# Two chunks of one batch, instead of one chunk of two batches, in the first paired tiles of a linear attention with a gated feed-forward on one core

## The chip, the core and the metric

The kernel runs on one core of a Trainium2 chip. The metric is the device time of one execution in microseconds (us). A profile is one execution recorded by the hardware profiler; its span runs from the first to the last instruction.

## What is computed

The reference has two parts. The first is a linear attention with a decaying state, for 4 batches, 8 heads, 768 tokens and a head dimension of 48:

```python
for t in range(S):
    cur = np.einsum('bhd,bhe->bhde', u[None] * kt, vt)
    y[:, :, t] = np.einsum('bhd,bhde->bhe', rt, state + cur)
    state = wt[:, :, :, None] * state + np.einsum('bhd,bhe->bhde', kt, vt)
```

The second takes the 3072 rows of 384 values that this gives, scales each by its root mean square and a gain, and computes `(silu(xn @ w_gate) * (xn @ w_val)) @ w_out` with an inner width of 1536. Everything comes and goes as float32.

## The kernel before, in words

**Tiles.** The 768 tokens of a batch are cut into 6 chunks of 128. A tile (n, j) is chunk n of batch j: 24 tiles. For each tile the attention is done in matrix form: the logarithms of the decay are summed along the tokens with a triangular matrix (`cs_mm`), the sums are exponentiated (`exp_r`, `exp_k`), r and k are multiplied by them (`r_mul`, `k_mul`) into the buffer `rk`, `rk` is transposed (`rk_pe` on TensorE and `rk_tr`, a copy out of PSUM; or a transposing DMA from chunk 2 on), a score matrix is formed (`q_mm`), masked (`q_mask_e`, `q_mask_o`), and multiplied by v (`y_mm`), together with the state that the chunks before left (`st_mm`, `st_new`). A term for the token itself (`bonus_mul`, `bonus_sum`, `bonus_v`, mostly GpSimd's work) is added in `x_add`. `x_sq`, `x_rstd`, `xn_mul` normalise the row, `xn_pe` and `xn_out` transpose it into `xnt`, the input of the feed-forward.

**Feed-forward.** Four tiles make one group of 512 tokens. A group has 12 units; each is a `gate_mm` and a `val_mm` (3 matmuls of 512 columns each, line 741), a `silu` on ScalarE, and an `h_mul` on VectorE into `ht`. Then come four `o_mm` of 12 matmuls (line 784), `o_out` and `out_dma`. In the groups of the tuple `HALF` (0 and 1) a unit is computed for two tiles at a time: 6 matmuls of 256 columns (line 746), so that it needs only half of the group's tiles. The table `COL` says which tile has which place in which group: group 0 holds chunks 0 and 1 of batches 0 and 1.

**Pairs.** The four tiles in `PAIR` = (0,0), (0,1), (1,0), (1,1) are laid out specially. The loaded data of chunk n of batches 0 and 1 lie in one tile: batch 0 on partitions 0 to 63, batch 1 on 64 to 127, two neighbouring tokens on a partition, so that a descriptor moves 384 bytes instead of 192. Each load (`load` line 276, `load_w` line 298) therefore fills 64 partitions, and it takes two for each of w, r, k and v of a chunk: 16 loads of 192 KB. All later tiles load 128 partitions with 192-byte rows (lines 280 and 298), and w of chunks 0 and 1 of batches 2 and 3 (`WIN`) two tokens a partition on 128 partitions, 384 KB at once.

**Order.** One string, `ORDER`, lists all steps as name.n.j; the program issues them in that order, and every engine works through its own part strictly in sequence. All loads are on SyncE's (SP's) queue. The weights `wg_sb` and `wv_sb` (in two parts: units 0 to 3, and units 4 to 11) and `wo` are loaded by GpSimd's queue (lines 394 and 399). PSUM is used in rings: two banks for gate and for the sums of r ("a"), two for val and the sums of k ("b"), four for the rest ("q").

Of the kernel before, what the change touches and what calls it, by code (L numbers as in the profile page):

```python
# [25 lines left out]
u_mm.0.0 load_w.0.1 load_w.0.0 load_r.0.0 load_k.1.0 load_k.0.1 load_r.0.1 ln.0.0 u_out.0.0 cs_mm.0.1 load_k.0.0  # L26
exp_r.0.1 cs_mm.0.0 load_w.1.0 load_w.1.1 load_r.1.0 load_k.1.1 exp_k.0.1 exp_r.0.0 r_mul.0.1 exp_k.0.0 bonus_mul.0.1
bonus_mul.0.0 ln.1.0 k_mul.0.1 r_mul.0.0 w_tot.0.0 w_tot.0.1 k_mul.0.0 rk_pe.0.1 g_mm.0.0 rk_pe.0.0 cs_mm.1.0
load_r.1.1 rk_tr.0.1 exp_r.1.0 load_v.0.1 load_w.0.3 load_v.0.0 cs_mm.1.1 load_w.0.2 exp_k.1.0 rk_tr.0.0 bonus_sum.0.1
r_mul.1.0 exp_r.1.1 exp_k.1.1 g_out.0.0 w_tot.1.1 k_mul.1.0 q_mm.0.0 bonus_mul.1.1 k_mul.1.1 load_gv.0.1 q_mask_e.0.0  # L30
rk_pe.1.0 q_mm.0.1 ln.0.3 load_v.1.0 load_v.1.1 load_k.0.3 load_r.0.3 bonus_mul.1.0 bonus_sum.0.0 r_mul.1.1 cast_v.0.1
cast_v.0.0 q_mask_o.0.0 q_mask_o.0.1 q_mask_e.0.1 cs_mm.0.3 bonus_v.0.0 st_mm.0.0 st_mm.0.1 rk_pe.1.1 st_new.0.0
bonus_v.0.1 y_mm.0.0 ln.0.2 rk_tr.1.0 rk_tr.1.1 w_tot.1.0 st_new.0.1 load_gv.0.0 bonus_sum.1.0 x_add.0.0 bonus_sum.1.1
y_mm.0.1 load_r.0.2 exp_r.0.3 q_mm.1.1 cast_v.1.0 cast_v.1.1 x_sq.0.0 x_rstd.0.0 w_tot.0.3 x_add.0.1 q_mm.1.0
bonus_v.1.0 load_gv.1.0 q_mask_e.1.1 q_mask_o.1.1 bonus_v.1.1 xn_mul.0.0 x_sq.0.1 exp_k.0.3 load_k.0.2 cs_mm.0.2
st_mm.1.0 q_mask_e.1.0 q_mask_o.1.0 xn_pe.0.0 y_mm.1.1 r_mul.0.3 exp_r.0.2 x_rstd.0.1 xn_mul.0.1 exp_k.0.2 xn_out.0.0
xn_pe.0.1 w_tot.0.2 x_add.1.1 load_v.0.2 bonus_mul.0.3 k_mul.0.3 x_sq.1.1 y_mm.1.0 x_rstd.1.1 xn_out.0.1 load_gv.1.1
x_add.1.0 load_w.2.0 load_k.1.2 xn_mul.1.1 load_r.1.2 r_mul.0.2 st_new.1.0 load_v.0.3 x_sq.1.0 load_w.2.2 x_rstd.1.0
bonus_mul.0.2 gate_mm.0.0 rk_pe.0.3 st_mm.1.1 xn_pe.1.1 val_mm.0.1 k_mul.0.2 gate_mm.0.1 rk_pe.0.2 xn_mul.1.0
load_r.1.3 load_v.1.2 load_k.1.3 silu.0.1 silu.0.0 rk_tr.0.3 xn_pe.1.0 val_mm.0.0 cast_v.0.2 load_w.2.1 gate_mm.0.3  # L40
# [80 lines left out]
gate_mm.5.9 val_mm.5.2 val_mm.5.4 gate_mm.5.5 h_mul.5.2 silu.5.5 silu.5.9 o_out.4.3 val_mm.5.9 out_dma.4.2 h_mul.5.4  # L121
val_mm.5.5 gate_mm.5.7 gate_mm.5.10 h_mul.5.9 h_mul.5.5 out_dma.4.3 val_mm.5.7 silu.5.7 silu.5.10 val_mm.5.10
h_mul.5.7 o_out.4.1 h_mul.5.10 o_mm.5.0 o_mm.5.3 o_mm.5.2 o_out.5.3 o_mm.5.1 o_out.5.0 out_dma.5.3 out_dma.5.0
out_dma.4.1 o_out.5.2 out_dma.5.2 o_out.5.1 o_mm.5.4 out_dma.5.1 o_out.5.4 out_dma.5.4
"""


@with_exitstack
def kernel(
# [13 lines left out]
    nc = tc.nc  # L143
# [700 lines left out]
```

## Time and profile before

| | |
|---|---|
| time, median of 3 runs | 205.45 us (204.31 to 205.63) |
| time of the profiled execution | 204.67 us |
| its span | 203.0 us |
| busy: PE, VectorE (DVE), ScalarE (ACT), GpSimd (POOL) | 189.7, 155.5, 137.7, 123.2 us |
| mean granted TensorE clock | 0.991 |
| DMA traffic | 32.44 MB, mean 160 GB/s |

In the profile PE is TensorE's matmul stream; matmuls are pipelined, so the time between the starts of two of them is the price of one, and not the duration that is shown. `ps_au`, `ps_qx` and so on are PSUM banks of the rings a, b and q. In the chain of waits each row is a piece of the work that ended last: start, length, what. In a timeline row the square bracket says how long the engine had been idle before it and what released it.

### The profile page before, as it was taken

To read this page: it belongs to the slowest core of one execution; us is meant where nothing else is said; L and a number is where in the kernel's file an instruction comes from. 1 tells how busy PE (TensorE), PEld (TensorE's weight loads), DVE (VectorE), ACT (ScalarE), POOL (GpSimd) and SP (SyncE) were. 2 spreads that over 40 slices of the span, in tenths; PEclk is the share of its full clock that TensorE was granted. 3 is DMA by queue.
4 is the path that set the end of the run, shared out by engine and by line. 5 is a ranking of instruction groups with operands and counts; after the bars stand their busy time and mean duration, and the time that the engine had idled before them with its cause. 6 is when DMAs were issued, how large, how long until landed. Compare 5 with 4: busy or idle time off the path is not lost.

```text
span 203.0 us, 4914 instructions
## 1 busy us (share of the span) xinstructions
PE 189.7 (93%) x1832; PEld 128.2 (63%) x1832; DVE 155.5 (77%) x304; ACT 137.7 (68%) x282; POOL 123.2 (61%) x178
## 2 busy tenths in 40 slices
PE   2798779999999999999999997999999999999993
PEld 0356569989768999765556663556655565555562
DVE  6279896799988999988999987899898892044611
ACT  2547996689988667988598969667886484063500
POOL 7299992294639985486998198558797474300000
PEclk9999988999999999999999999999999999999999
DMA  5999999999999999999999989991367112001122
GB/s 121 218 226 248 192 209 211 188 196 168 210 208 204 183 208 210 191 214 204 235 204 204 207 202 211 217 185 39 100 111 196 39 30 72 19 17 63 39 97 99
DMA packets 115520, 32.44 MB, mean 160 GB/s; under 512 B 110372, under 2 KB 114344, under 8 KB 115496
## 3 DMA queue, kind: packets, MB, share of 16 engines
q1 hardware_dynamic: 113456, 28.58, 68.4%
q0 software_dynamic: 2032, 3.54, 10.0%
q8 instruction: 14, 0.23, 0.5%
q14 instruction: 10, 0.08, 0.1%
q10 hardware_dynamic: 8, 0.00, 0.0%
HBM read 25.96 MB, written 4.72 MB: 151 GB/s over the span
## 4 chain that ended last, share of the span: by engine, by line
PE 62%; DMA 13%; POOL 10%; ACT 6%; SPq 5%; issue 3%; POOLq 0%; ACTq 0%
PE ps_au L741 6%; PE ps_av L741 6%; PE ps_bu L741 5%; PE ps_bv L741 5%; PE ps_qz L784 5%; PE ps_av L746 4%; PE ps_au L746 4%; DMA wt<-in_w_dram 4%; PE ps_qx L784 4%; PE ps_qv L784 4%; PE ps_bu L746 4%; POOL ruk L535 4%; PE ps_bv L746 3%; DMA wg_sb<-in_moe_w_gate_dram 3%; POOL ruk L536 3%; PE ps_qu L784 3%
## 5 line engine op out<-in xcount | busy, mean ns | idle before, releaser
L784 PEld LDWEIGHTS <-ht 128*128 128x128 bf16 x300 | 28.5, 98 | 17.0
L253 ACT ACTIVATE sg<-ps_au 128x512 bf16<-128x512 f32 x35 | 20.9, 598 | 16.9 <-PE ps_au L741 9.1
L253 ACT ACTIVATE sg<-ps_av 128x512 bf16<-128x512 f32 x37 | 22.1, 596 | 15.1 <-PE ps_av L741 12.8
L770 DVE TENSOR_TENSOR ht<-ps_bu,sg 128x512 bf16<-128x512 f32 x24 | 16.5, 686 | 14.0 <-PE ps_bu L741 10.9
L536 POOL TENSOR_TENSOR ruk<-ruk,u_bc 128x384 f32<-128x384 f32 x24 | 24.3, 1011 | 1.9
L741 PEld LDWEIGHTS <-wg_sb 128*128 128x128 bf16 x144 | 15.5, 114 | 14.1 <-issue 1.6
L741 PEld LDWEIGHTS <-wv_sb 128*128 128x128 bf16 x144 | 15.5, 114 | 13.0
L741 PE MATMUL ps_av<-xnt,wg_sb 128*128 128x512 bf16 x75 | 20.3, 379 | 1.3 <-ACT sg L253 1.3
L770 DVE TENSOR_TENSOR ht<-ps_bv,sg 128x512 bf16<-128x512 f32 x24 | 16.4, 685 | 6.3 <-PE ps_bv L741 3.9
L545 POOL TENSOR_TENSOR ydiag<-vt,diag 128x384 f32<-128x384 f32 x20 | 16.5, 831 | 7.3 <-DVE diag L540 5.4
L535 POOL TENSOR_TENSOR ruk<-rt,kt 128x384 f32<-128x384 f32 x20 | 20.0, 1002 | 0.2 <-DMA rt<-in_r_dram 0.2
L741 PE MATMUL ps_bu<-xnt,wv_sb 128*128 128x512 bf16 x72 | 19.5, 380 | 0.0
L741 PE MATMUL ps_bv<-xnt,wv_sb 128*128 128x512 bf16 x72 | 19.5, 380 | 0.0
L784 PE MATMUL ps_qv<-wo,ht 128*128 128x384 bf16 x108 | 19.0, 326 | 0.0
L741 PE MATMUL ps_au<-xnt,wg_sb 128*128 128x512 bf16 x69 | 18.7, 380 | 0.0
L253 ACT ACTIVATE lw<-wt 128x384 bf16<-128x384 f32 (+1 forms) x20 | 11.5, 583 | 7.8 <-DMA wt<-in_w_dram 7.8
L251 ACT ACT_TABLE_LOAD x12 | 15.4, 1283 | 1.8 <-PEq L828 1.6
L529 POOL TENSOR_TENSOR rk<-kt,ek 128x384 bf16<-128x384 f32 x15 | 15.2, 1024 | 2.3 <-DMA kt<-in_k_dram 2.3
L746 PEld LDWEIGHTS <-wg_sb 128*128 128x128 bf16 x144 | 15.5, 115 | 1.5 <-DMA wg_sb<-in_moe_w_gate_dram 0.9
L746 PEld LDWEIGHTS <-wv_sb 128*128 128x128 bf16 x144 | 15.2, 114 | 0.4
L695 ACT ACTIVATE xn<-xb,rstd 128x384 bf16<-128x384 f32 x24 | 14.3, 611 | 1.0 <-POOL rstd L691 0.8
L682 ACT ACTIVATE junk<-xb 128x384 bf16<-128x384 f32 x24 | 12.4, 518 | 1.7 <-DVE xb L677 1.5
(210 smaller groups left out, 445.4 us busy)
## 6 DMA issues: line engine op xcount, KB each, us to landing
wt<-in_w_dram SPq DMA_DIRECT2D x20, 192.0 KB, 3.8
kt<-in_k_dram SPq DMA_DIRECT2D x20, 192.0 KB, 3.8
rt<-in_r_dram SPq DMA_DIRECT2D x20, 192.0 KB, 4.3
vt<-in_v_dram SPq DMA_DIRECT2D x20, 192.0 KB, 3.8
out_dram<-ob SPq DMA_DIRECT2D x19, 192.0 KB, 2.2
wo<-in_moe_w_out_dram POOLq DMA_DIRECT2D x3, 384.0 KB, 6.7
out_dram<-ob SPq DMA_DIRECT2D x10, 96.0 KB, 2.8
ht<-in_r_dram SPq DMA_DIRECT2D x4, 192.0 KB, 5.0
```

The source lines that it names most:

```text
L251: nc.scalar.preload_act_table_set(table_name)
L253: return nc.scalar.activation(**kw).ins
L529: eng.tensor_tensor(out=rk[:, n % 2, j, 1, :, 0:D], in0=arr("k", n, j), in1=bank["cs_k", n, j][:, 0:DM].rearrange("p (h d) -> p h d", h=H) ...
L535: nc.gpsimd.tensor_tensor(out=ruk[n, j], in0=arr("r", n, j), in1=arr("k", n, j), op=ALU.mult)
L536: nc.gpsimd.tensor_tensor(out=ruk[n, j], in0=ruk[n, j], in1=u_bc, op=ALU.mult)
L545: nc.gpsimd.tensor_tensor(out=ydiag[n, j], in0=arr("v", n, j), in1=diag[n, j].to_broadcast([128, H, D]), op=ALU.mult)
L682: nc.scalar.activation(out=junk, in_=xb[n, j], func=AF.Square, accum_out=rstd[n, j][:, 0:1])
L695: nc.scalar.activation(out=xn, in_=xb[n, j], func=AF.Copy, scale=rstd[n, j][:, 1:2])
L741: nc.tensor.matmul(ps, lhsT=units(ws, c, f), rhs=x[:, c, :], start=(c == 0), stop=(c == KC - 1))
L746: nc.tensor.matmul(ps[:, i * TS // 2:(i + 1) * TS // 2], lhsT=units(ws, c, f + i), rhs=x[:, c, cols], start=(i == 0 and c == 0), stop=(i = ...
L770: nc.vector.tensor_tensor(out=ht[n][:, f, :], in0=v, in1=sg, op=ALU.mult)
L784: nc.tensor.matmul(ps[:, cols], lhsT=ht[n][:, f, b * L:(b + 1) * L], rhs=wo_of["wo"][:, f, cols], start=(f == 0), stop=(f == FC - 1))
```

## The change

The four paired tiles are laid out the other way round. A loaded tile now holds 256 tokens of one batch, chunk 0 on partitions 0 to 63 and chunk 1 on partitions 64 to 127, two neighbouring tokens a partition. Each of w, r, k, v of a batch is one load of 128 partitions and 384 KB: 8 loads instead of 16. Chunk 1's output now needs the state after chunk 0 on half of its partitions, so all four `y_mm` have 4 matmuls with the state (before, 8 in each of chunk 1's two and none in chunk 0's); their number is unchanged, as is that of `cs_mm`, `q_mm`, `st_mm`. The four tiles in `WIN` become eight, which only means that w of the pairs is loaded and its logarithm taken by the same code. `HALF` loses group 0: each of its 24 `gate_mm` and `val_mm` is 3 matmuls of 512 columns instead of 6 of 256, so that 72 matmuls and 72 weight loads go (3660 rows on TensorE become 3516). The output of a paired tile is stored by one DMA of 128 partitions instead of two of 64. `ORDER` is a new list throughout, and the sets that choose an engine for a step are new: VectorE has one instruction less, GpSimd eleven more, ScalarE 14 table loads instead of 12.

```diff
 ORDER = """
-u_mm.0.0 load_w.0.1 load_w.0.0 load_r.0.0 load_k.1.0 load_k.0.1 load_r.0.1 ln.0.0 u_out.0.0 cs_mm.0.1 load_k.0.0
+load_w.0.0 ln.0.0 u_mm.0.0 cs_mm.0.0 exp_r.0.0 cs_mm.1.0 load_k.0.0 load_r.0.0 u_out.0.0 bonus_mul.1.0 exp_k.0.0
...
-    WIN = sel("02 03 12 13")
+    WIN = sel("00 01 02 03 10 11 12 13")
     PAIR = sel("00 01 10 11")
...
-    COL = {(0, 2): (1, 0), (1, 2): (1, 1), (0, 3): (1, 2), (1, 3): (1, 3), (1, 0): (0, 2), (1, 1): (0, 3)}
-    HALF = (0, 1,)
+    COL = {(0, 2): (1, 0), (1, 2): (1, 1), (0, 3): (1, 2), (1, 3): (1, 3), (1, 0): (0, 1), (0, 1): (0, 2), (1, 1): (0, 3)}
+    HALF = (1,)
...
     def load(which, n, j):
         t = {"r": r, "k": k, "v": v}[which]
         if (n, j) in PAIR:
...
-            b = j % 2
-            nc.sync.dma_start(out=o[b * PD:(b + 1) * PD].rearrange("p h i d -> p h (i d)"),
-                              in_=t[j, :, n * L:(n + 1) * L, :].rearrange("h (p i) d -> p h (i d)", i=2))
+            o = inp[which, 0, j] = inp[key][:, int(which == "k"), j]
+            nc.sync.dma_start(out=o.rearrange("p h i d -> p h (i d)"),
+                              in_=t[j, :, 0:2 * L, :].rearrange("h (p i) d -> p h (i d)", i=2))
             return
...
     def cs_mm(n, j):
...
-                nc.tensor.matmul(o, lhsT=mp[:, int(x < i)], rhs=lw[:, n % 2, j0 + x, :, 0:D], start=(x == 0),
-                                 stop=(i == 1 and x == 1))
+                nc.tensor.matmul(o, lhsT=mp[:, int(x < n)], rhs=lw[:, x, j, :, 0:D], start=(x == 0),
+                                 stop=(n == 1 and x == 1))
...
     def y_mm(n, j):
...
-            if n > 0:
-                for i in range(NP):
-                    for b in range(2):
-                        nc.tensor.matmul(ps[halves[b], i * 2 * D:(i + 1) * 2 * D], lhsT=inp["rkT"][:, n, i, x, halves[b]],
-                                         rhs=st[:, n % 2, j0 + b, i, :], start=(i == 0), stop=False)
+            lo, hi = halves
+            for i in range(NP):
+                nc.tensor.matmul(ps[hi, i * 2 * D:(i + 1) * 2 * D], lhsT=inp["rkT"][:, j, i, n, hi],
+                                 rhs=st[:, 1, j, i, :], start=(i == 0), stop=False)
...
     def out_dma(n, j):
...
-            for b in range(2):
-                row0 = (j - j % 2 + b) * S + i * L
-                nc.sync.dma_start(out=out[row0:row0 + L].rearrange("(p a) m -> a p m", a=2)[j % 2],
-                                  in_=bank[ob][b * PD:(b + 1) * PD])
+            nc.sync.dma_start(out=out[j * S:j * S + 2 * L].rearrange("(p a) m -> a p m", a=2)[i], in_=bank.pop(ob))
```

How the instructions stand on an engine is shown at three places. The first is the start of SP's queue, that is, the order of the loads. In these rows `ht` and `wo` are the buffers in which r and k, and v, of the pairs lie (they are later used for the feed-forward); `wt`, `rt`, `kt`, `vt` are the buffers of all other tiles. Before:

```order
L298 DMA wt<-in_w_dram 64x8x96 x2
L276 DMA ht<-in_r_dram 64x8x96
L276 DMA ht<-in_k_dram 64x8x96 x2
...
L276 DMA ht<-in_k_dram 64x8x96
L298 DMA wt<-in_w_dram 64x8x96 x2
...
L276 DMA wo<-in_v_dram 64x8x96
L298 DMA wt<-in_w_dram 128x8x96
```

And now:

```order
L288 DMA wt<-in_w_dram 128x8x96
L272 DMA ht<-in_k_dram 128x8x96
L272 DMA ht<-in_r_dram 128x8x96
...
L272 DMA wo<-in_v_dram 128x8x96
L288 DMA wt<-in_w_dram 128x8x96 x2
L276 DMA rt<-in_r_dram 128x8x48
L272 DMA wo<-in_v_dram 128x8x96
L276 DMA kt<-in_k_dram 128x8x48 x2
```

The first three loads now bring all of w, k and r that batch 0's two paired tiles need; the next three do so for batch 1. Batch 1's v has moved behind w of batches 2 and 3.

The second place is GpSimd, where the weights of the feed-forward are issued among its products (`ruk` is r times k times u, `ydiag` the token's own term; `wg_sb0` and `wv_sb0` hold units 0 to 3, `wg_sb4` and `wv_sb4` units 4 to 11). Before:

```order
L529 TENSOR_TENSOR rk_110<-ht_150,ek_261 128x8x48
L394 DMA wv_sb0_143<-in_moe_w_val_dram 128x3x512
L535 TENSOR_TENSOR ruk_327<-ht_150 128x384
L536 TENSOR_TENSOR ruk_327<-ruk_327,u_bc_76 128x384
L545 TENSOR_TENSOR ydiag_354<-wo_242,diag_330 128x384
L545 TENSOR_TENSOR ydiag_384<-wo_242,diag_257 128x384
L394 DMA wg_sb0_141<-in_moe_w_gate_dram 128x3x512
L434 CAST vb_487<-wo_242 128x384
L545 TENSOR_TENSOR ydiag_518<-wo_242,diag_426 128x384
L394 DMA wg_sb4_142<-in_moe_w_gate_dram 128x3x1024
```

And now:

```order
L515 TENSOR_TENSOR rk_110<-ht_172,ek_299 128x8x48
L521 TENSOR_TENSOR ruk_328<-ht_172 128x384
L522 TENSOR_TENSOR ruk_328<-ruk_328,u_bc_76 128x384
L531 TENSOR_TENSOR ydiag_359<-wo_190,diag_288 128x384
L384 DMA wg_sb4_142<-in_moe_w_gate_dram 128x3x1024
L531 TENSOR_TENSOR ydiag_362<-wo_190,diag_213 128x384
L424 CAST vb_450<-wo_190 128x384
L598 AFFINE_SELECT qts_439<-qts_439 64x512 x2
L531 TENSOR_TENSOR ydiag_494<-wo_190,diag_357 128x384
L531 TENSOR_TENSOR ydiag_496<-wo_190,diag_297 128x384
L384 DMA wv_sb4_144<-in_moe_w_val_dram 128x3x1024
```

The two large parts now come first, and the two small ones ten instructions after them; the first `gate_mm` of the program uses `wg_sb4`, where it used `wg_sb0`.

The third place is VectorE around the last of the four `xnt` of group 0, with the first `ht` product of the feed-forward behind it. Before:

```order
L720 TENSOR_TENSOR xnt_611<-ps_qz_613,gT_77 128x3x128
L677 TENSOR_TENSOR xb_674<-ps_qu_629,ydiag_518 128x384
L523 TENSOR_TENSOR rk_110<-rt_465,ps_au_533 128x8x48
L642 TENSOR_TENSOR ps_qx_547<-ps_qx_547,st_113 128x384
L643 TENSOR_TENSOR st_113<-ps_qx_547,wcol_422 128x384
L529 TENSOR_TENSOR rk_110<-kt_531,ek_609 128x8x48
L568 COPY rkT_764<-ps_qv_705 128x1024
L720 TENSOR_TENSOR xnt_611<-ps_qu_723,gT_77 128x3x128
L720 TENSOR_TENSOR xnt_611<-ps_qv_766,gT_77 128x3x128
```

And now:

```order
L655 TENSOR_TENSOR xb_648<-ps_qv_564,ydiag_496 128x384
L655 TENSOR_TENSOR xb_650<-ps_qz_601,ydiag_494 128x384
L698 TENSOR_TENSOR xnt_692<-ps_qu_664,gT_77 128x3x128
L551 COPY rkT_694<-ps_qz_677 128x1024
L698 TENSOR_TENSOR xnt_692<-ps_qx_658,gT_77 128x3x128
L698 TENSOR_TENSOR xnt_692<-ps_qu_697,gT_77 128x3x128
L698 TENSOR_TENSOR xnt_692<-ps_qz_701,gT_77 128x3x128
```

Before, six other instructions stood between the second `xnt` and the third, and the feed-forward began after the second. Now the four stand together, and the feed-forward needs all of them.

More of the change, by code (lines that the diff above doesn't have):

```diff
@@ L36 @@
[L36 to L40, printed above, removed]
@@ L256 @@
     inp = {}
+    halves = [slice(c * PD, (c + 1) * PD) for c in range(2)]
     def arr(which, n, j):
[L259 to L262 removed]
+        return inp[which, 0, j][:, :, n] if (n, j) in PAIR else inp[which, n, j]
     def load(which, n, j):
```

302 lines of the change are left out of this document (142 added, 160 removed).

## The prediction

> **What bounds the kernel now.** I read the page first, then the chain of waits, then the timelines of the first 35 us. The page:
>
> ```profile
> span 203.0 us, 4914 instructions
> PE 189.7 (93%) x1832; PEld 128.2 (63%) x1832; DVE 155.5 (77%) x304; ACT 137.7 (68%) x282; POOL 123.2 (61%) x178
> PE   2798779999999999999999997999999999999993
> ```
>
> PE is busy in nine tenths or more of nearly every slice after the sixth (one slice is 5.1 us). Busy alone proves little with pipelined matmuls, so I look at what ends PE's idle time. The list of waits, for PE, has after the start only these two that matter:
>
> ```profile
> PE ps_av L741 <- ACT sg L253: 1.3, 1, 1.3
> PE ps_av L746 <- DMA wg_sb<-in_moe_w_gate_dram: 0.8, 1, 0.8
> ```
>
> So from the first `gate_mm` to the last `o_mm` PE has its next matmul nearly always ready. The chain of waits gives the place where that begins, and the price of a unit of work:
>
> ```profile
> 22.17 6.32 DMA wg_sb<-in_moe_w_gate_dram
> 28.53 1.47 PE ps_av L746 x6
> 33.34 0.45 PE ps_qx L552 x8
> 34.61 0.66 PE ps_au L746 x6
> 125.91 0.65 PE ps_au L741 x3
> ```
>
> The span is therefore a thin stage of 28.5 us, in which loads and the first tiles' chains decide, and a dense one of 174.5 us, in which PE's work decides. A change pays if the dense stage begins earlier or has less left to do. The first unit took 1.47 instead of 0.66 us: PE's clock had fallen.
>
> ```profile
> 28.00:30.00 2.00, 1.47 (x8) 1.08 (x9) 1.97 (x5) 1.87 (x7) 1.98 (x3) 0.62 1.12 200
> 30.00:32.00 2.00, 2.00 (x21) 1.65 (x20) 1.70 (x2) 1.75 (x2) 1.88 (x2) 0.52 1.13 203
> ```
>
> Of these windows the last three columns are granted clock, DMA share and GB/s: at 0.62 and 0.52 for 4 us, (0.38 + 0.48) x 2 = 1.7 us are lost. The new order has the same thin PE work ahead of its dense stage, so I leave this loss in.
>
> **The dense stage.** *Fewer matmuls:* a unit of 6 costs 0.66, of 3 0.65 us: 24 x 0.01 = 0.2 us less. *Moved work:* since the feed-forward must wait for four tiles instead of two, PE does more before it. Ahead of the first `gate_mm` now also stand `rk_pe`.0.2 (8 transposes, 0.45 above), `q_mm`.0.2, one `st_mm` and two `xn_pe`:
>
> ```profile
> 24.39 0.51 PE L632 MATMUL ps_qx<-vb,rk 64*128 64x96 bf16 x8
> 24.84 0.34 PE L710 MATMUL ps_qu<-ident,xn 128*128 128x128 bf16 x3
> 33.63 0.33 PE L710 MATMUL ps_qv<-ident,xn 128*128 128x128 bf16 x3
> 33.80 0.82 PE L746 MATMUL ps_bu<-xnt,wv_sb 128*128 128x256 bf16 x6
> 96.05 0.23 PE L592 MATMUL ps_qx<-rkT 48*128 48x128 bf16 x1
> 96.82 0.84 PE L741 MATMUL ps_bu<-xnt,wv_sb 128*128 128x512 bf16 x3
> ```
>
> From start to start, `st_mm` is 0.45 (24.39 to 24.84), `xn_pe` 0.17 (33.63 to 33.80), and two `q_mm` 0.77 (96.05 to 96.82). Together 0.45 + 0.38 + 0.45 + 0.34 = 1.6 us. So after the first `gate_mm` there are 1.8 us less to do, and the span changes by (new start of the dense stage - 28.5) - 1.8. Equal span: a start at 30.3.
>
> **The loads.** A load of 64 partitions against one of 128, in windows where mostly one kind moves (last column GB/s; 14.7 and 17.1 are the two 384 KB loads of w that already fill 128 partitions):
>
> ```profile
> 8.00:10.00 2.00, 1.54 (x16) 0.70 (x13) 0.55 (x1) 1.17 (x3) 0.00 (x0) 1.00 1.30 218
> 12.00:14.00 2.00, 2.00 (x20) 1.32 (x18) 1.39 (x3) 0.88 (x2) 1.92 (x3) 1.00 1.32 207
> 14.70:15.90 1.20, 1.20 (x26) 0.72 (x25) 1.20 (x5) 0.95 (x3) 1.12 (x2) 1.00 1.21 304
> 17.10:18.30 1.20, 0.76 (x12) 0.59 (x12) 1.20 (x3) 1.04 (x3) 1.20 (x2) 1.00 1.21 304
> ```
>
> The 16 small loads are 3.15 MB: at 213 GB/s 14.8 us, at 304 10.3, so 4.4 us less of a queue that is full from 2.4 us on. The Trainium skill has a rule for this: its page "SBUF — State Buffer", section "Door 1: The DMA port swizzle (why `[64,N]` ≈ `[32,N]`)", says that 64 partitions reach only half of the memory's 16 ports, 196 against 328 GB/s at 1 MiB. The trace agrees in kind, with 213 against 304 GB/s; by the page's rates the 16 loads would gain 6.4 us (an estimate).
>
> **The start of the dense stage,** in four legs, from these rows (a window, then the timelines of SP, ACT, DVE and POOL):
>
> ```profile
> 2.00:4.00 2.00, 0.41 (x1) 0.41 (x2) 1.68 (x2) 0.90 (x1) 1.73 (x8) 1.00 0.72 188
> 0.79 1.45 SPq L298 DMA_DIRECT2D wt<-in_w_dram  x2
> 5.36 0.84 ACT L253 ACTIVATE lw<-wt 128x768 bf16<-128x768 f32 x1 [2.45 <-DMA wt<-in_w_dram]
> 9.22 0.47 ACT L253 ACTIVATE ps_bv<-ps_bv 128x384 f32<-128x384 f32 x1 [0.18 <-PE ps_bv L461]
> 16.64 0.84 ACT L253 ACTIVATE lw<-wt 128x768 bf16<-128x768 f32 x1 [0.84 <-DMA wt<-in_w_dram]
> 20.57 1.02 ACT L562 COPY ht<-ps_qx 128x1024 bf16<-128x1024 bf16 x1
> 9.03 0.55 DVE L523 TENSOR_TENSOR rk<-ht,ps_au 128x384 bf16<-128x384 f32 x1 [3.20 <-ACT ps_av L253]
> 10.01 1.42 POOL L535 TENSOR_TENSOR ruk<-ht 128x384 f32<-128x384 f32 x1 [3.46 <-DMA ht<-in_k_dram]
> 16.69 0.54 DVE L523 TENSOR_TENSOR rk<-ht,ps_av 128x384 bf16<-128x384 f32 x1
> 22.49 0.55 DVE L677 TENSOR_TENSOR xb<-ps_qz,ydiag 128x384 f32<-128x384 f32 x1
> 22.95 0.68 DVE L602 TENSOR_TENSOR qts<-ps_qx,mq 128x512 bf16<-128x512 f32 x1
> 23.55 0.68 DVE L610 TENSOR_TENSOR qts<-ps_qu,mq 128x512 bf16<-128x512 f32 x1
> 26.91 0.56 DVE L720 TENSOR_TENSOR xnt<-ps_qz,gT 128x384 bf16<-128x384 bf16 x1
> 34.00 0.56 DVE L720 TENSOR_TENSOR xnt<-ps_qv,gT 128x384 bf16<-128x384 bf16 x1 [1.37 <-PE ps_qv L710]
> ```
>
> *Leg 1, the first loads.* Data begin to move at about 2.4 us (188 GB/s in the window 2 to 4 us). Each 384 KB takes 1.3 us at 304 GB/s; from the last byte to the waiting engine it was 0.74 us (15.90 to 16.64). So w is there at 4.5 to 4.9, k at 6.0, r at 7.2; then VectorE's `r_mul` and GpSimd's first product start, instead of at 9.03 and 10.01. With no gain in the rate it would be 9.0.
>
> *Leg 2, the second tile.* ScalarE takes the logarithm of batch 0 at 4.7 and, as from 5.36 to 9.69, 4.3 us later has done its four exponentials: 9.0. Batch 1's w came at 8.0 and waits. Its logarithm, four exponentials and, between them, a copy of 1.0 us (the 20.57 row): the third exponential ends at about 13.6, and `r_mul`.1.1 can start. Before, its like started at 16.69. Bounds: 13.1, and 15.4 with leg 1 at its worst.
>
> *Leg 3, VectorE.* From there to the fourth `x_add` it has 22 instructions: 12 at 0.46 (22.49 to 22.95), 7 at 0.60 (22.95 to 23.55), 3 of eight columns at 0.1: 10.1 us, and some 1 us of waits: 24.7. GpSimd's `ydiag` come in time: from 7.2 it has ten products at 1.0 us (row below), the issue of `wg_sb4`, then a cast, two masks and three more products of at most 1.0: the last is done by 23.
>
> *Leg 4, the normalisation.* From `x_add` to `xnt` the second tile took 26.91 + 0.56 - 22.49 - 0.55 = 4.4 us, with ScalarE at other things in between. Now two tiles go through ScalarE together with nothing else: I take 4.0, bounds 3.0 and 4.4. The fourth `xnt` ends at 28.7, where before it ended at 34.56.
>
> The weights for the first unit are hidden behind this: `wg_sb4` is issued after ten of GpSimd's products, at about 17.4, and lands within the 9.2 us of the row below, at 26.6. `wv_sb4` is issued at about 23 and lands by 32.5; PE needs it after four units, a transposition and the clock's loss, 28.8 + 2.6 + 0.5 + 1.7 = 33.6, with 1.1 us to spare.
>
> ```profile
> wg_sb<-in_moe_w_gate_dram POOLq DMA_DIRECT2D x1, 768.0 KB, 9.2
> wv_sb<-in_moe_w_val_dram POOLq DMA_DIRECT2D x1, 768.0 KB, 9.5
> L536 POOL TENSOR_TENSOR ruk<-ruk,u_bc 128x384 f32<-128x384 f32 x24 | 24.3, 1011 | 1.9
> L251 ACT ACT_TABLE_LOAD x12 | 15.4, 1283 | 1.8 <-PEq L828 1.6
> ```
>
> **The rest of the edits** I cost at nothing, with their cover: two more table loads are 2.6 us of ScalarE, which is busy 68%; before, one of twelve loads stopped PE (the 1.3 us above), so two more are worth 0.2, at most 2.6. Eleven more instructions on GpSimd (61% busy) lie behind PE's queue of units. Twelve fewer DMAs shorten SP's queue only, and later loads come up to 4.4 us earlier than now, when PE hardly waits for them. The end, four `o_mm` and their stores, is the same.
>
> **Sum:** 28.8 - 28.5 - 1.8 = -1.5 us: span 201.5. With the 1.67 us around it the profiled execution's 204.67 becomes 203.2. That run is 0.8 under the median of the three shown, against which 203.2 is 1.1% less; against its own time it is 0.7% less. The start of the dense stage by the legs' bounds lies between 26.2 (13.1 + 10.1 + 3.0) and 31.6 (15.4 + 11.8 + 4.4): 200.6 to 206.0. If the 1.3 us wait goes too, 199.3; if the table loads cost all of 2.6, 208.6.
>
> **The rivals.** *B, the whole gain in loading reaches the feed-forward:* VectorE, whose 36 instructions from the 9.03 row to the 26.91 row take 18.4 us with 2.2 of waits, is kept filled by data that come in time, and the dense stage starts at 26.3. For it: GpSimd and VectorE both began by waiting for data, 3.5 and 3.2 us. Against it: leg 2 is ScalarE's own work. 204.67 - 2.2 - 1.8 = 200.7, faster.
>
> *C, the change does not do what it says:* the three first loads move no faster than now, because in the first 2 us loads to both halves are in the queue together. Then leg 1 ends at 9.0, the start is 30.6, and the time 205.0: no change.
>
> *D, the fourth tile takes the place of the weights:* the feed-forward waits for a tile that is late. The row at 34.00 speaks for it: this is where the fourth `xnt` is now, and it must come 5.8 us forward. Against it: six instructions that stood ahead of it on VectorE stand elsewhere. PE then idles, and the price is one for one: slower by 1% from a start at 32.4, and with the fourth `xnt` where it is now, 34.6 - 28.5 - 1.8 = 4.3 us, 209.0. If `wv_sb4` is late by several us, it is the same price at the next unit.
>
> **How the numbers follow.** 1% is 2 us, about what a measurement of this kernel can tell from no change. The forecast, 203.2 with its own range of 201.6 to 204.9, gets 0.50; B 0.24, C 0.13, D 0.13. Of the forecast's cases two fifths lie beyond 1%: faster 0.20 + 0.24 = 0.44. Slower is D, and some of it stays under 1%: 0.12, with 0.02 for table loads that all stop PE: 0.14. The rest, 0.42, is within 1%. The range goes from 200.3, below B, to 206.3, which leaves out most of D.
>
> **What would show it.** Right: the three first loads done by 7.5 us and GB/s near 300 before 10 us; GpSimd's first product at about 7; VectorE with 1 to 2 us of waits from 13.6 to 24.7; the first `gate_mm` at 28 to 30, released by the fourth `xnt`; the units behind it back to back. Wrong: a first `gate_mm` after 31; PE waiting for `wv_sb`; waits of PE on `sg` or `ht` of more than 2 us in all; loads near 215 GB/s in the first 10 us.

## The result, and the profile after

| | before | after |
|---|---|---|
| time, median of 15 executions | 205.48 us (203.86 to 206.62) | 202.70 us (201.01 to 208.5) |
| time of the profiled execution | 204.67 us | 203.7 us |
| its span | 203.0 us | 201.9 us |

The ratio is 0.987, with a 95% interval from 0.983 to 0.990: the change makes the kernel 1.3% faster, about 2.7 us. Single executions on some chips are held up by several us; all ratios here leave those out.

The page of the changed kernel, its first line, the busy times, and PE's busy tenths:

```profile
span 201.9 us, 4738 instructions
PE 187.6 (93%) x1744; PEld 120.4 (60%) x1760; DVE 155.4 (77%) x303; ACT 136.8 (68%) x277; POOL 129.5 (64%) x189
PE   2979979999999999999999999699999999999993
```

As before, PE is busy in nearly every slice, but there is a new dent, a 6, in the slice from 126 to 131 us. The windows of the changed kernel (busy time and count of PE, PEld, DVE, ACT, POOL, then granted clock, DMA share, GB/s):

```profile
2.00:4.00 2.00, 0.41 (x1) 0.41 (x2) 1.68 (x2) 0.90 (x1) 1.73 (x8) 1.00 0.93 241
4.00:6.00 2.00, 2.00 (x10) 0.59 (x10) 1.33 (x3) 0.84 (x1) 1.82 (x4) 1.00 1.17 324
8.00:10.00 2.00, 1.54 (x11) 1.08 (x10) 1.97 (x6) 1.23 (x3) 2.00 (x2) 1.00 1.17 325
28.00:30.00 2.00, 1.95 (x10) 1.01 (x9) 1.17 (x3) 0.81 (x2) 1.17 (x2) 0.57 1.13 203
30.00:32.00 2.00, 2.00 (x11) 1.07 (x10) 1.32 (x3) 0.79 (x2) 1.92 (x3) 0.58 1.08 212
```

The loads run at 320 to 325 GB/s from 4 to 12 us, where the narrow ones ran at 207 to 218 in the windows that the prediction shows, and the clock falls after the start of the feed-forward as it did before. The legs of the start, from the timelines of ACT, DVE, POOL and PE:

```profile
4.31 0.84 ACT L253 ACTIVATE lw<-wt 128x768 bf16<-128x768 f32 x1 [1.40 <-DMA wt<-in_w_dram]
6.82 0.55 DVE L509 TENSOR_TENSOR rk<-ht,ps_au 128x384 bf16<-128x384 f32 x1 [0.99 <-DMA ht<-in_r_dram]
6.87 1.00 POOL L521 TENSOR_TENSOR ruk<-ht 128x384 f32<-128x384 f32 x1 [0.32 <-DMA ht<-in_r_dram]
13.12 0.56 DVE L509 TENSOR_TENSOR rk<-ht,ps_au 128x384 bf16<-128x384 f32 x1 [0.24 <-ACT ps_au L253]
23.56 0.56 DVE L655 TENSOR_TENSOR xb<-ps_qz,ydiag 128x384 f32<-128x384 f32 x1 [0.26 <-PE ps_qz L640]
27.02 0.56 DVE L698 TENSOR_TENSOR xnt<-ps_qz,gT 128x384 bf16<-128x384 bf16 x1
27.63 0.85 PE L719 MATMUL ps_au<-xnt,wg_sb 128*128 128x512 bf16 x2
17.34 0.98 POOL L384 DMA_DIRECT2D wg_sb<-in_moe_w_gate_dram  x1
22.65 0.81 POOL L384 DMA_DIRECT2D wv_sb<-in_moe_w_val_dram  x1
```

The fourth `xnt` ends at 27.58 and the first `gate_mm` starts at 27.63, 0.9 us earlier than before, though it now waits for four tiles. What PE waited for after the start:

```profile
PE ps_qz L574 <- DMA rkT<-rk: 2.3, 1, 2.3
PE ps_qx L574 <- DMA rkT<-rk: 0.3, 1, 0.3
```

Both are `q_mm` of chunk 4 waiting for a transposing DMA; the kernel before had no such wait on its list, but one of 1.3 us for `sg` at 125 us, which is gone. How far each kernel is, from the timelines of PE (start of the first `gate_mm`, and of the first `o_mm` of each group; the lower rows are experiments):

```
                        gate    o_mm of group 0     1      2      3      4      5    span
before                  28.53              53.6   81.8  111.8  141.6  168.5  191.8   203.0
after                   27.63              50.9   78.7  108.8  140.5  167.2  190.5   201.9
after_third (same)      27.55              52.1   80.0  111.9  141.4  168.2  191.5   202.9
after_halves            27.33              50.4   78.3  110.6  139.4  166.1  189.5   200.8
after_64_second         30.37              57.2   85.1  116.5  147.2  174.0  197.3   209.1
after_tr_first          27.53              50.8   78.6  108.7  138.0  164.7  188.0   199.4
after_all_tr_wo         27.57              50.7   78.5  108.6  137.5  164.2  187.5   198.9
best_64                 31.35              54.4   82.3  112.4  140.8  167.5  190.8   202.6
```

The row after_third is the same kernel in another execution; it shows how far two executions lie apart. At group 0 the change is 2.7 us ahead: 0.9 by the start and 1.8 by the work left after it. It is 3.0 ahead at group 2 and 1.1 at group 3: 1.9 us are given back between these two rows of `o_mm`.

### The profile page after: what moved, and what is told of

It reads as the page before. It is cut to its first block, busy times and chain, and to the rows that moved or that the text cites. A ratio compares the mean times of both kernels' runs of the same rounds, so it can differ in the third digit from the quotient of the medians.

```text
span 201.9 us, 4738 instructions
## 1 busy us (share of the span) xinstructions
PE 187.6 (93%) x1744; PEld 120.4 (60%) x1760; DVE 155.4 (77%) x303; ACT 136.8 (68%) x277; POOL 129.5 (64%) x189
## 4 chain that ended last, share of the span: by engine, by line
PE 78%; ACT 8%; DMA 3%; DVE 3%; issue 3%; POOL 3%; POOLq 0%; ACTq 0%
PE ps_bv L719 9%; PE ps_av L719 9%; PE ps_bu L719 9%; PE ps_au L719 9%; PE ps_qx L762 6%; PE ps_qu L762 6%; PE ps_qv L762 4%; PE ps_qz L762 3%; DMA rkT<-rk 3%; PE ps_bv L724 2%; PE ps_bu L724 2%; PE ps_au L724 2%; PE ps_av L724 2%; ACT junk L660 2%; ACT xn L673 1%
## 5 line engine op out<-in xcount | busy, mean ns | idle before, releaser
L719 PEld LDWEIGHTS <-wg_sb 128*128 128x128 bf16 x180 | 19.7, 115 | 16.7 <-issue 1.1
L719 PEld LDWEIGHTS <-wv_sb 128*128 128x128 bf16 x180 | 19.1, 114 | 15.4
L748 DVE TENSOR_TENSOR ht<-ps_bv,sg 128x512 bf16<-128x512 f32 x30 | 20.6, 688 | 8.8 <-PE ps_bv L719 6.8
L719 PE MATMUL ps_av<-xnt,wg_sb 128*128 128x512 bf16 x88 | 24.9, 388 | 0.1
L719 PE MATMUL ps_au<-xnt,wg_sb 128*128 128x512 bf16 x86 | 24.5, 389 | 0.2
L719 PE MATMUL ps_bu<-xnt,wv_sb 128*128 128x512 bf16 x88 | 24.3, 380 | 0.2
L719 PE MATMUL ps_bv<-xnt,wv_sb 128*128 128x512 bf16 x82 | 23.7, 380 | 0.4
L762 PE MATMUL ps_qu<-wo,ht 128*128 128x384 bf16 x84 | 14.8, 326 | 0.0
L762 PE MATMUL ps_qv<-wo,ht 128*128 128x384 bf16 (+1 forms) x84 | 13.8, 314 | 0.0
L526 DVE TENSOR_REDUCE diag<-ruk 128x8 f32<-128x384 f32 x24 | 13.0, 544 | 0.9 <-POOL ruk L522 0.9
```

The lines of the kernel that those rows point to most:

```text
L719: nc.tensor.matmul(ps, lhsT=units(ws, c, f), rhs=x[:, c, :], start=(c == 0), stop=(c == KC - 1))
L748: nc.vector.tensor_tensor(out=ht[n][:, f, :], in0=v, in1=sg, op=ALU.mult)
L762: nc.tensor.matmul(ps[:, cols], lhsT=ht[n][:, f, b * L:(b + 1) * L], rhs=wo_of["wo"][:, f, cols], start=(f == 0), stop=(f == FC - 1))
```

## The experiments

Twelve runs follow, two of them of the changed kernel as it is and ten of nine kernels that alter it. The theory: 128-partition loads bring the start forward, PE turns an earlier start and less remaining work into time one for one, and the transposing DMAs give part of it back. The rivals: the new order, or the group in one piece, is what pays; or the transfers are hidden.

### The changed kernel again (after_again, after_third)

No edit.

> The changed kernel as it is, a second execution. In the first profile PE waited 2.26 us at 131.6 us and 0.32 us at 123.1 us for a transposing DMA (rkT). Theory: this wait belongs to the order of SP's queue, so it stands here again, 1.5 to 2.5 us, and the first gate_mm starts again at 27.4 to 27.9. Rival: it is an accident of that one execution, because its span of 201.9 was the longest of the undisturbed ones; then it is under 0.5 us here and the span is near 200.5.

> The changed kernel as it is, a third execution, on the same chip as the three kernels after it. In the two profiles so far PE waited for rkT 2.26 + 0.32 us and 1.39 + 0.61 us before q_mm of chunk 4; with group 0 in halves it was 2.06 us in chunk 3 and 0.32 in chunk 4. Theory: between 1.0 and 2.7 us of such waits in chunks 3 and 4 together; ratio to the kernel before 0.985 to 0.989. Rival (the waits are an accident): none over 0.3 us.

The ratios were 0.985 (0.976 to 0.995) and 0.989 (0.984 to 0.995). PE waited for `rkT` 1.4 + 0.6 us in the one profile and 2.7 us in the other, there 1.57 in chunk 3 and 1.10 in chunk 4. The wait belongs to the order; its size and its place change from execution to execution. Both of these executions show a second one, which the first did not have: PE waits for `rk` of tile (1,3). PE's row for it in after_again:

```profile
PE ps_qv L538 <- POOL rk L515: 4.0, 1, 4.0
```

And in after_third, from PE's list of waits, POOL's timeline, and the DMA times of tile kt:

```profile
PE ps_qz L574 <- DMA rkT<-rk: 2.7, 2, 1.6
PE ps_qv L538 <- POOL rk L515: 1.1, 1, 1.1
```

```profile
45.08 0.99 POOL L515 TENSOR_TENSOR rk<-kt,ek 128x384 bf16<-128x384 f32 x1 [2.92 <-DMA kt<-in_k_dram]
```

```profile
DMA to landing us min/median/max: 3.5/4.1/12.4
```

GpSimd's `k_mul` of tile (1,3) waited 2.9 us for its k, whose load took 12.4 us where the median is 4.1, and PE waited 1.1 us for GpSimd. In after_again the load took 14.7 us and PE waited 4.0, and the granted clock was 0.50 to 0.51 from 48 to 54 us: its first `o_mm` came at 57.1.

### Narrow loads put back (after_64_loads, after_64_second)

```diff
-            nc.sync.dma_start(out=o.rearrange("p h i d -> p h (i d)"),
-                              in_=t[j, :, 0:2 * L, :].rearrange("h (p i) d -> p h (i d)", i=2))
+            for b in range(2):
+                nc.sync.dma_start(out=o[b * PD:(b + 1) * PD].rearrange("p h i d -> p h (i d)"),
+                                  in_=t[j, :, b * L:(b + 1) * L, :].rearrange("h (p i) d -> p h (i d)", i=2))
```

The same is done for w.

> The changed kernel with its eight 384 KB loads of w, r, k, v of the four paired tiles cut into two of 64 partitions each, lower half first; layout, order and all else as in the changed kernel. Theory (the rate of the loads sets the start, and PE turns a later start into a later end one for one): about 213 GB/s instead of 324 in the windows from 4 to 12 us, VectorE's first product at 8.8 to 9.2 instead of 6.82, r_mul.1.1 at 14.5 to 15.4 instead of 13.12, the first gate_mm at 29.0 to 29.8 instead of 27.63, and the time 1.4 to 2.2 us over the changed kernel. Rival (the gain comes from the new order and from work moved ahead of the feed-forward; the transfers are hidden): first gate_mm within 0.5 us of 27.63, time within 0.5 us of the changed kernel's.

> The changed kernel with its eight 384 KB loads cut into sixteen of 64 partitions, again, beside the changed kernel on one chip. The first profile of it had the first gate_mm at 30.39 instead of 27.63 and 231 to 240 GB/s instead of 320 to 325. Theory: the same start within 0.3 us, the o_mm of groups 0 to 2 later by the same 2.4 to 3.0 us, and the time 2.0 to 3.0 us over the changed kernel's, so at or above that of the kernel before less 0.8. Rival (the dense stage has slack that takes up a later start): the o_mm of group 2 less than 1 us later, and the time within 1 us.

Windows of the first of them, and its timelines of DVE:

```profile
4.00:6.00 2.00, 1.29 (x3) 0.24 (x3) 1.31 (x3) 0.84 (x1) 1.82 (x4) 1.00 1.08 233
8.00:10.00 2.00, 1.37 (x8) 0.54 (x7) 1.12 (x4) 1.06 (x3) 1.00 (x2) 1.00 1.29 237
10.00:12.00 2.00, 1.13 (x7) 0.65 (x7) 2.00 (x5) 0.84 (x1) 2.00 (x2) 1.00 1.29 231
```

```profile
8.88 0.55 DVE L514 TENSOR_TENSOR rk<-ht,ps_au 128x384 bf16<-128x384 f32 x1 [3.06 <-DMA ht<-in_r_dram]
15.40 0.56 DVE L514 TENSOR_TENSOR rk<-ht,ps_au 128x384 bf16<-128x384 f32 x1 [0.48 <-ACT ps_au L253]
29.77 0.56 DVE L703 TENSOR_TENSOR xnt<-ps_qz,gT 128x384 bf16<-128x384 bf16 x1
```

VectorE's first product is at 8.88 instead of 6.82, `r_mul`.1.1 at 15.40 instead of 13.12, and the first `gate_mm` at 30.39 and 30.37 instead of 27.6: the first two within the theory's bounds, the last 0.6 us beyond them, although the loads ran at 231 to 248 GB/s in the two runs, and not at 213. So the transfers are not hidden. The first run has no ratio (206.2 to 213.1 us); the second gave 1.012 (1.004 to 1.019) against the kernel before, beside 0.989 for the changed kernel on the same chip: 2.2%, some 4.5 us. That is more than the 2 to 3 us expected, and the `o_mm` of groups 0 to 2 came 4.6 to 5.1 us later than in after_third, where 2.4 to 3.0 were expected. Its profile has more in it than the later start: PE waited 2.4 us for `rk` of tile (1,3) and 3.3 us for `rkT`, where after_third has 1.1 and 2.7, and the granted clock fell to 0.50 once more from 50 to 52 us, behind the wait for `rk`. To price the loads alone these waits had to go first.

The Trainium skill's page "SBUF — State Buffer", section "Door 1: The DMA port swizzle (why `[64,N]` ≈ `[32,N]`)", gives 328 GB/s for 128 partitions and 196 for 64. The 324 GB/s here agree with the first; 231 to 248, with both halves following each other in the queue, and 207 to 218 before, lie above the second.

### Group 0 in halves (after_halves)

```diff
-    HALF = (1,)
+    HALF = (0, 1,)
```

and the units of group 0 renamed in `ORDER`, so that the first ones use the weights that come first.

> The changed kernel with group 0 of the feed-forward in halves again (HALF = (0, 1)): 6 matmuls of 256 columns for each gate_mm and val_mm instead of 3 of 512, 72 matmuls and 72 weight loads more; the units are renamed so that those of the large weight parts come first, and all steps stand where they stood. Theory: the price is 24 x 0.01 = 0.2 us, first gate_mm where it is (27.6). Rival (the one-piece group is where the dense stage became shorter): 24 x 0.08 = 1.9 us or more, as much as the whole gain of the dense stage.

The ratio was 0.979 (0.973 to 0.986), beside 0.985 of the changed kernel on that chip. From the first `gate_mm` to the first `o_mm` PE took 50.4 - 27.33 = 23.1 us, with the group in one piece 50.9 - 27.63 = 23.3. So the 72 matmuls and weight loads saved are worth nothing that shows, and the rival's 1.9 us are not there. In this execution the wait for `rkT` stood in chunk 3 (2.06 us at 102 us).

### Transposing DMAs ahead of the next chunk's loads (after_tr_first, after_all_tr)

SP's queue around chunk 4 in the changed kernel:

```profile
118.29 2.68 SPq L549 DMA_TRANSPOSE rkT<-rk  x2
121.02 0.59 SPq L276 DMA_DIRECT2D kt<-in_k_dram  x1
121.64 1.74 SPq L276 DMA_DIRECT2D rt<-in_r_dram  x2
123.49 0.64 SPq L782 DMA_DIRECT2D out_dram<-ob  x1
124.30 3.00 SPq L549 DMA_TRANSPOSE rkT<-rk  x1
127.35 0.58 SPq L288 DMA_DIRECT2D wt<-in_w_dram  x1
128.05 1.45 SPq L549 DMA_TRANSPOSE rkT<-rk  x1
```

The last transposition is the one that PE waits for. Its input was ready at 124.75 (VectorE's `k_mul`.4.2), it was issued at 128.05, and PE's weight load that waited for it started at 131.60. In between the queue, which has no gap here, was at the transposition before it (3.0 us for an instruction that takes 1.26 at the median) and a load of w. The edit, as it stands in SP's queue:

```diff
+L782 DMA out_dram<-ob 128x384
+L549 DMA_TRANSPOSE rkT<-rk 128x8x128 x2
 L276 DMA kt<-in_k_dram 128x8x48
 L276 DMA rt<-in_r_dram 128x8x48 x2
-L782 DMA out_dram<-ob 128x384
-L549 DMA_TRANSPOSE rkT<-rk 128x8x128
 L288 DMA wt<-in_w_dram 128x8x48
-L549 DMA_TRANSPOSE rkT<-rk 128x8x128
```

after_all_tr does the same with the other transpositions of chunks 3 and 4, most of all

```diff
-L288 DMA wt<-in_w_dram 128x8x48 x3
 L549 DMA_TRANSPOSE rkT<-rk 128x8x128
 L288 DMA wt<-in_w_dram 128x8x48
 L549 DMA_TRANSPOSE rkT<-rk 128x8x128
+L288 DMA wt<-in_w_dram 128x8x48 x3
```

> The changed kernel with SP's queue turned round at one place: the transposing DMAs rk_tr.4.3 and rk_tr.4.2 stand ahead of five others, the loads of k and two of r and one of w of chunk 5 among them, and not behind them; all other engines as they are. Theory (the 2.26 us wait of PE before q_mm.4.2 is the transposition being late behind SP's other DMAs, and nothing else is near it): rkT of tile (4,2) is issued at about 126 and lands by 129.2, PE waits for it under 0.3 us, the o_mm of group 3 start 2.0 us or more earlier, and the time is 1.5 to 2.3 us less than the changed kernel's. Rival 1 (the limit is k_mul.4.2, which VectorE ends only at 124.75, and the 3 us of the transposition itself): the wait shrinks by less than 1 us. Rival 2 (the moved loads of chunk 5 become the next late thing): the wait at 131.6 goes, another for wt or kt comes behind it, and the time stays within 0.5 us.

> The changed kernel with only SP's queue reordered: in chunks 3 and 4 the transposing DMAs stand ahead of the loads of the next chunk that stood ahead of them (three loads of w in chunk 3; two of r, two of k and one of w in chunk 4). Turning round two of them took the profiled span to 199.4 with 0.58 us of waits left. Theory (the waits are SP's queue of loads ahead of the transpositions): no wait of PE for rkT over 0.3 us in either chunk, time 1.5 to 2.6 us under the changed kernel's. Rival (what is late is rk itself, from k_mul, or the moved loads become late): a wait of 1 us or more for rkT, rk or wt stays, and the time is within 1 us of the changed kernel's.

The first gave 0.973 (0.966 to 0.980), with the changed kernel at 0.985 on the same chip, and the `o_mm` of group 3 came at 138.0 instead of 140.5. The second gave 0.967 (0.962 to 0.973), with the changed kernel at 0.989. The first has 0.6 us of waits for `rkT` left, the second has none on its list. So it was SP's queue, not `k_mul`, and the moved loads did not become late. The gain of the first over the changed kernel, 1.2% or 2.5 us, is about what was expected, though the two intervals overlap. That of the second, 2.2% or 4.5 us, is more than the 1.5 to 2.6 expected and more than the 2.7 us that PE waited for `rkT` in after_third; no run shows what the rest is. What the second still has is the other wait (PE's list):

```profile
PE ps_qv L538 <- POOL rk L515: 1.5, 1, 1.5
```

### The late k of tile (1,3) (after_k13, after_all_tr_k13, after_all_tr_wo)

In the first two, the loads of k and r of tile (1,3) stand ahead of the two loads of w of chunk 2:

```diff
+L276 DMA kt<-in_k_dram 128x8x48
+L276 DMA rt<-in_r_dram 128x8x48
 L288 DMA wt<-in_w_dram 128x8x48 x2
-L276 DMA rt<-in_r_dram 128x8x48
-L276 DMA kt<-in_k_dram 128x8x48
```

> The changed kernel with one step of SP's queue turned round: the loads of k and r of tile (1,3) ahead of the two loads of w of chunk 2, not behind them. In four executions of kernels with the changed order PE waited 1.1 to 4.0 us at 46 to 50 us for rk of tile (1,3), which GpSimd could not make because its k landed up to 12 to 14 us after its issue, while GpSimd's queue brought the late feed-forward weights; in three others it did not wait. Theory (k is issued next to the weights and shares the DMA engines with them): issued some 4 us earlier it is there by 41 us, PE never waits for rk there, the executions lie closer together, and the time is 0 to 1.5 us under the changed kernel's; the waits for rkT at 95 to 133 us stay (1.0 to 2.7 us). Rival (the DMA engines are simply full from 26 to 46 us, whatever stands first): the wait moves to w of chunk 2 or to v, and the time stays.

> Both reorderings of SP's queue together: the transposing DMAs of chunks 3 and 4 ahead of the next chunk's loads, and k and r of tile (1,3) ahead of w of chunk 2. Theory: no wait of PE over 0.5 us between 30 and 196 us, span 198.0 to 199.0, time 199.5 to 200.7, 2 to 3 us under the changed kernel's, and no execution with a hole at 46 us. Rival (another late load takes the place): a wait of 1 us or more after 30 us.

after_k13 gave 0.986 (0.981 to 0.991), no gain that can be told from the changed kernel's 0.985 to 0.989 on other chips. Its profile has no wait for `rk`, but 1.3 us for `rkT`, and its executions did not lie closer together (201.0 to 207.9 us). With the transpositions moved as well it was 0.976 (0.970 to 0.981), 199.75 to 201.84 us. The profile answers to the rival; it is of the longest of the six executions, and the other five lie within the 199.5 to 200.7 expected. ACT's timeline, and PE's list of waits:

```profile
45.20 0.52 ACT L253 ACTIVATE lw<-wt 128x384 bf16<-128x384 f32 x1 [2.04 <-DMA wt<-in_w_dram]
```

```profile
PE ps_av L719 <- ACT sg L253: 1.0, 1, 1.0
```

Here w of chunk 2 is late, ScalarE waits 2.0 us for it with `silu` queued behind, and PE 1.0 us for `silu`: in this execution the order of SP's loads only chose who was late. The profile's page counts the packets of SP's and of GpSimd's queue against the same 16 DMA engines (68.0 and 9.8% of them in the changed kernel), and on GpSimd's queue the change issues `wo` from 34 us on; before it was 43 to 48. So the last kernel leaves SP's loads alone, keeps the transpositions moved, and moves two loads of `wo` in GpSimd's queue:

```diff
 L384 DMA wv_sb_143<-in_moe_w_val_dram 128x3x512
-L389 DMA wo<-in_moe_w_out_dram 128x1536
...
-L389 DMA wo<-in_moe_w_out_dram 128x1536
+L389 DMA wo<-in_moe_w_out_dram 128x1536 x2
```

(The one between them now brings the first part instead of the second.)

> The kernel with the transposing DMAs of chunks 3 and 4 ahead of the next chunk's loads, and with two steps of GpSimd's queue moved: the first two of the three loads of wo, issued at 34 and 38 us in the changed kernel (before the change all three were issued from 43 to 48), stand 4 to 10 us later; SP's loads of k and r of tile (1,3) are where the change put them. Theory (the hole of 0 to 4 us at 46 to 50 us comes from GpSimd's weights, which move beside SP's loads; putting k first only handed the delay to w of chunk 2): with 0.39 to 0.79 MB less ahead of them, k of tile (1,3) is there by 43 us and w of chunk 2 too, PE waits for neither over 0.5 us, wo is there for the o_mm at 50.5, the span is 198.0 to 199.0 and the time 199.5 to 200.7. Rival 1 (SP's queue alone makes k late): a wait of 1 us or more for rk of tile (1,3) stays. Rival 2 (wo becomes the late one): PE waits 1 us or more at the first o_mm.

It gave 0.963 (0.957 to 0.969) and a span of 198.9. GpSimd's two `k_mul` in its timeline, the DMA times of tile kt, and the end of PE's list of waits (all rows are of the thin stage but the one for wcol):

```profile
41.04 1.97 POOL L515 TENSOR_TENSOR rk<-kt,ek 128x384 bf16<-128x384 f32 x2 [2.21 <-ACT ek L253]
```

```profile
DMA to landing us min/median/max: 3.2/3.9/8.5
```

```profile
PE ps_av L468 <- DVE wcol L504: 0.3, 1, 0.3
PE ps_qz L688 <- ACT xn L673: 0.2, 1, 0.2
PE ps_qu L635 <- DVE st L625: 0.2, 1, 0.2
```

Both `k_mul` run back to back, waiting for ScalarE and not for a load, and PE waits nowhere over 0.31 us after the feed-forward has begun. This version beats the kernel before by 3.7%, and its interval lies below those of the changed kernel, measured on other chips. But it does not show that `wo` is what makes k late. The first profile of the changed kernel, with `wo` where the change put it, has the same rows:

```profile
41.23 1.98 POOL L515 TENSOR_TENSOR rk<-kt,ek 128x384 bf16<-128x384 f32 x2 [2.21 <-ACT ek L253]
DMA to landing us min/median/max: 3.2/3.9/7.2
```

Nine profiles are of kernels that leave both this k and `wo` where the change put them. In five of them PE waits 1.1 to 4.0 us for `rk`, and the longest load of tile kt took 12.2 to 14.7 us; in the other four (after, after_halves, after_tr_first, after_warm_early) there is no such wait, and it took 5.4 to 9.1. One profile without the wait is therefore what the unmoved `wo` gives nearly half the time. Nor does the time show a gain: the executions behind the ratio took 199.7 to 201.0 us, those of after_all_tr 199.7 to 200.9. What delays k in some executions stays open. The Trainium skill's page "DMA: Bandwidth & Descriptors", section "Queues, rings and completion order", says that each DMA engine takes turns between the queues, a packet at a time. By that rule weights on one queue can delay loads on the other; no run here shows the turns.

### Narrow loads without the later waits (best_64)

The narrow loads from above in the kernel after_all_tr_k13.

> The kernel with both reorderings, and with the loads of the paired tiles cut into sixteen of 64 partitions. Here the later waits for k and rkT are out of the way, so that the price of narrow loads stands alone. Theory: first gate_mm at 30.3 to 30.5, 2.7 to 3.0 us later, the o_mm of groups 0 to 5 later by the same 2.5 to 3.2, and the time 2.5 to 3.2 us over that of the kernel with both reorderings. Rival 1 (narrow loads cost more than their start, since they push all later loads back): 4 us or more, with new waits after 30 us. Rival 2 (the dense stage takes the later start up): under 1.5 us.

The ratio was 1.001 (0.996 to 1.005), beside 0.976 with wide loads on the same chip: 2.5%, about 5 us. Its profile, of its quickest execution (204.3 us), has no wait of PE after the start, so that it can be laid beside after_all_tr_wo, which has none either: the start is 3.8 us later (31.35 against 27.57), the `o_mm` of groups 0, 1 and 2 3.7 to 3.8, of groups 3 to 5 3.3, and the span 3.7. PE turned the later start into a later end one for one. The theory's mechanism holds, and its size was too small: the start moved by 2.8, 2.8 and 3.8 us in three executions, where I had written 1.4 to 2.2 at first. The extra 1.0 us of the third arises later than `r_mul`.1.1, which stands at 15.28, as in the other two (15.40 and 15.16); its cause is open, and so is why the ratios differ by 5 us and the two profiles by 3.7. Of rival 1 there is the price but not the new waits.

### More work for PE early (after_warm_early)

```diff
-load_w.0.0 ln.0.0 u_mm.0.0 cs_mm.0.0 exp_r.0.0
+load_w.0.0 ln.0.0 u_mm.0.0:14 cs_mm.0.0:8 exp_r.0.0
```

(The number is that of added matmuls on zeros.)

> The changed kernel with 22 matmuls of 384 columns on a tile of zeros more, ahead of u_mm.0.0 and of cs_mm.0.0, where PE waits for the first load (1 to 5.4 us); their result is overwritten. The granted clock falls to 0.57 and 0.58 in the windows from 28 to 32 us, just after the feed-forward begins, which costs (0.43 + 0.42) x 2 = 1.7 us. Theory 1 (the fall follows PE's first stretch of full work, wherever that lies): the clock falls at 4 to 10 us, where PE is not the bound, stays at 1.00 from 28 to 32, and the time is up to 1.7 us less. Theory 2 (the fall follows the step from thin to dense work at 27.6): clock and time as in the changed kernel, within 0.5 us.

Its windows, of which the third column from the end is the granted clock:

```profile
16.00:18.00 2.00, 2.00 (x19) 1.32 (x18) 2.00 (x5) 1.40 (x2) 1.92 (x3) 0.50 0.81 158
18.00:20.00 2.00, 2.00 (x41) 1.66 (x40) 0.63 (x2) 1.09 (x2) 1.97 (x4) 0.71 0.91 178
30.00:32.00 2.00, 1.58 (x11) 0.87 (x12) 2.00 (x6) 0.00 (x0) 0.28 (x1) 0.50 1.14 215
32.00:34.00 2.00, 2.00 (x9) 0.92 (x8) 0.48 (x2) 0.82 (x2) 1.44 (x2) 0.50 0.95 186
34.00:36.00 2.00, 2.00 (x10) 0.99 (x9) 1.34 (x3) 0.77 (x2) 1.92 (x4) 0.50 0.87 174
```

Theory 1 fell: the clock did not stay at 1.00 from 28 to 32 us, and no time was gained. The ratio was 0.995 (0.992 to 0.999), beside 0.989 (0.984 to 0.995) of the changed kernel on the same chip; the intervals touch. Theory 2 does not fit this profile either. The clock fell a first time at 16 to 20 us, some eight microseconds after the last added matmul (7.9 us), and then again when the feed-forward began, longer than without it, and the first `gate_mm` started at 31.0 instead of 27.6. This is one profile, of an execution of 207.3 us.

Nor does the fall always follow the step to dense work. In after_64_loads the granted clock was 1.00 in every window from 2 to 48 us, and fell only from 48 to 56, behind the 4.0 us in which PE waited for `rk`; two of its windows:

```profile
30.00:32.00 2.00, 1.82 (x18) 1.18 (x16) 1.93 (x5) 1.36 (x3) 1.11 (x2) 1.00 1.11 204
50.00:52.00 2.00, 1.80 (x14) 0.98 (x15) 0.69 (x1) 0.00 (x0) 1.80 (x5) 0.50 1.02 201
```

What sets the fall off stays open.

## Why the prediction was right, and where it was not

The forecast was 203.2 us for an execution of 204.67, with a span of 201.5; the profiled one took 203.7 with 201.9. By its steps:

**The loads: right.** 304 GB/s were taken, 324 measured. (The estimate of 6.4 us given beside the 4.4 comes to 6.5 by its own figures; nothing rests on it.) That they count was the question between the forecast and the rival that transfers are no faster. Its start of 30.6 is what narrow loads gave (30.4, 30.4, 31.35), and its "no change" is the 1.001 of best_64: without the wide loads the rest of the change, even with SP's queue repaired, is worth nothing against the kernel before. The price was put too low, though: narrow loads cost 2.8 us or more of the start, where the two forecasts lie 1.8 apart (28.8 and 30.6).

**The four legs: right in kind, each a little too long.** Leg 1: 7.2 forecast, 6.82 measured. Leg 2: 13.6, measured 13.12. Leg 3: 11.1 us, measured 11.0 (13.12 to 24.12). Leg 4: 4.0, measured 24.12 to 27.58, 3.5. The start came at 27.6 instead of 28.8. The weights were issued at 17.3 and 22.7 (17.4 and 23 forecast) and were in time.

**The dense stage's 1.8 us: right.** From the first `gate_mm` to the first `o_mm` it was 53.6 - 28.53 = 25.1 us before and 23.3 after. Of its two terms the 0.2 for fewer matmuls does not show in after_halves, so the moved work, put at 1.6, would be all of the 1.8; a difference of 0.2 us between single executions settles neither. The clock's loss, left in at 1.7, was (0.43 + 0.42) x 2 = 1.7.

**"The rest at nothing": wrong.** The failed step is "Twelve fewer DMAs shorten SP's queue only, and later loads come up to 4.4 us earlier than now, when PE hardly waits for them". I counted the DMAs and not what stands behind them. The new order puts loads of the next chunk ahead of the transposing DMAs of chunks 3 and 4 that PE needs next. (The kernel before also has loads ahead of some of them, four loads ahead of the last one of chunk 4, but no such wait of PE.) PE then waited 2.6 us for `rkT` in the profiled execution, and 2.0 and 2.7 in the two others of the changed kernel. Moving those transpositions forward took the ratio from 0.985 to 0.973 and from 0.989 to 0.967, each on one chip, and removed most or all of the wait. The 1.1 and 4.0 us for a late k in two of the three executions are a second thing that the forecast did not have; their cause is not shown.

**The sum: right partly because errors cancel.** Against 201.5: start 1.2 earlier, the 1.3 us wait for `sg` gone (I had kept it in), 2.6 us of waits for `rkT` new: 201.6. The remaining 0.3 I have not placed. That the forecast came within 0.5 us of the profiled execution is partly luck in another way too. The medians differ by 2.8 us, nearly twice the 1.5 forecast, and the two profiled executions by 1.0, since the one before was quicker than its median and the one after slower than its own.

**The rivals.** The whole gain reaching the feed-forward would have been a start at 26.3: it was 27.6. The late fourth tile did not occur: the fourth `xnt` came 7 us earlier than before, as the six instructions ahead of it on VectorE were gone.

## What to carry to other kernels

A wide load pays where the engines of a thin first stage wait for data and the bounding engine starts behind them; then each microsecond of the start comes out at the end. When an order is rewritten, look at each queue for what now stands ahead of the few transfers that the bounding engine needs next (transpositions here), and not only at how many there are. When a wait comes and goes between executions of one kernel, a single profile without it says nothing for an edit: the late k was absent from four of nine profiles in which nothing had been done about it.

## What the runs showed of the hardware that I had not expected

- A transposing DMA held SP's queue 1.26 us at the median. In the first profile of the changed kernel two held it 3.0 and 3.3 us, with several loads directly ahead of them; in after_all_tr one held it 3.0 us with a single load of v directly ahead, so the number of loads does not settle it alone.
- The same load of 192 KB, in the same place of the same order, took 12.2 to 14.7 us in five profiles and at most 9.1 in four, where the median load of its kind takes 3.7 to 4.3.
- With 22 extra matmuls on zeros, from 1.0 to 7.9 us, the granted clock was 0.50 at 16 to 18 us (1.00 without them), and they did not spare the fall to 0.50 that follows the start of the dense stage.
- In the three profiles in which PE stood still 2.4 to 4.0 us for `rk` in the dense stage (after_again, after_64_loads, after_64_second), the granted clock fell to 0.50 behind it. It did not behind waits of 1.1 and 1.5 us for `rk` (after_third, after_all_tr), nor behind the 2.3 us for `rkT` in the first profile.
